# Windowed attention followed by a leaky-ReLU MLP on one core: second heads' dilated values of batch 0 issued by ScalarE, first w_in pieces cast by any of three engines, tables of order remade

## The chip, the core and the metric

The kernel runs on one core of one Trainium2 chip. The core has TensorE (PE, matrix products into PSUM banks), VectorE (DVE), ScalarE (ACT), GpSimd (POOL) and SyncE (SP), each with its own instruction stream in program order. SP, and here ACT too, also issue transfers from main memory. The metric is the device time of one execution in microseconds (us). Three runs of the kernel before gave 295.57, 295.67 and 296.05 us; their median, 295.67 us, is the time before. One more execution was taken with the hardware profiler on.

## What is computed

Attention over 8 batches of 8 heads, 576 positions, 64 values per head, in two kinds of mask, and then a two-layer MLP on the 4608 rows of 512 that come out:

```python
scores = scale * np.matmul(q, k.transpose(0, 1, 3, 2))
rel = pos[:, None] - pos[None, :]
mask_plain = (rel >= 0) & (rel < 32)                          # heads 0 to 3
mask_dil = (rel >= 0) & (rel < 128) & (rel % 4 == 0)          # heads 4 to 7
attn = softmax(np.where(masks, scores, -1e9))                 # last axis
x = np.matmul(attn, v).transpose(0, 2, 1, 3).reshape(4608, 512)
h = x @ w_in                                                  # 512 x 2048
g = np.maximum(0.01 * h, h)
out = g @ w_out                                               # 2048 x 512
```

Inputs and output are float32. The products run on float16 operands.

## The kernel before

**Tiling.** Heads are handled in pairs. A pair is a visit `vi`: visits 2 and 3 hold the dilated heads, 0 and 1 the plain ones, and every batch runs them in the order 2, 3, 0, 1. The two heads of a pair share a 128-partition tile: their keys and values stand in alternate columns of `slots`. A visit is split into two units (`unit`). A unit is a chain: scores on PE into a PSUM bank (`sps`, `ops`), Exp on ACT into `ee` (L904), row sums on PE by a block of ones (L921), Ln and Exp(-x) on ACT into `rc` (L940, L942), values on PE (L915), and a DVE multiply that writes the finished columns into `xt` (L953). For batches 0 and 1 the last 64 positions of all visits are one more unit, the rest unit (`rest_unit`, scores L994, Exp L1012, values L1000).

**Operands.** q, k and v are loaded as float32 into `stg` and `vst`, cast to float16 into `nat` or straight into `slots` (helper `cast`, recorded as L501 on ACT and L502 on DVE and POOL), turned by PE transposes (L740) for batches 0 and 1, and copied from PSUM into `slots` (helper `move`, L513 on ACT, L514 on DVE). The weight `w_in` comes in eight pieces w0 to w7 of 512 KB, one per visit and half of the 2048 columns, `w_out` in eight more, w8 to w15. Each piece is cast in two halves of 512 columns. Until they are cast the pieces stand in buffers that are needed later for something else (`gt`, `wst`, `xt`).

**MLP.** The first layer (`up`, L1054; two 192-column halves together in `up_pair`, L1088) sums four matmuls, one per visit, and ACT writes the leaky ReLU into `gt`. The second layer runs plain for four row tiles (L1268) and then as seven products instead of eight per group of four tiles (`group`, L1358). Chunks 9 to 11 run the first layer in the seven-product form too (L1188).

**What sets the order.** Every piece of work is recorded as a task with one engine or a choice of engines, estimated durations and dependencies. A planner (`_Plan`) schedules all tasks on a model of the machine, forward and backward, eight times, and keeps the best pass. Then each task's rank is moved by its number in `NUDGE`, some tasks are fixed to an engine by `HAND`, and one last forward pass gives the order in which the instructions are written out. `FIRST` sets the rank of the loads of batches 0 and 1 and of the weights. `ROOM`, `LATE`, `SOON`, `FAST` and `WHEN` are constants of the model. On the chip the engines follow the written order and wait for semaphores. Where the plan leaves PE idle before the first `up`, matmuls on the blank tile `warm` are put in (L1589).

**Loads.** `load_v(b, g, prio)` loads a half of the values of a batch: g = 1 the dilated heads, g = 0 the plain ones, `hh` is the first or second head of the pairs. For g = 1 each `hh` takes three transfers, two of 128 KB and one of 32 KB, for g = 0 one of 288 KB in 1152 pieces of 256 bytes. All of these are issued by SP; ACT issues the two halves of the dilated keys of batch 0 and the first constants (`con`). The completion of each transfer is counted on one of eight semaphores taken in turn over both queues, and the planner's model has the same limit:

```python
                    if eng == "SP":
                        here = max(here, landed[-8] if len(landed) >= 8 else 0.0)
```

so a transfer waits on its queue until the one eight places ahead of it in the written order has landed, and everything behind it on that queue waits too.

## Time and profile before

| | before |
|---|---|
| median of three runs | 295.67 us |
| the profiled execution's own time | 296.16 us |
| its span, first to last instruction | 294.4 us |
| PE busy | 284.7 us, 97% of the span |
| PE weight loads busy | 226.3 us, 77% |
| DVE busy | 225.3 us, 77% |
| ACT busy | 218.5 us, 74% |
| POOL busy | 124.2 us, 42% |
| mean granted PE clock | 0.994 of full speed |
| moved by DMA | 47.15 MB, 160 GB/s over the span |

The profile gives busy times per engine and per stretch of time (the windows view), the instructions in order of time (the timeline), who waited for whom (the waits view), groups of instructions of one kind, and the transfers with their time from issue to landing. Times in the views are microseconds from the start of the span; the span is 1.76 us shorter than the profiled execution's own time.

### The profile page before, as it was taken

The numbers are of one execution on the slowest core, as the hardware profiler recorded it, in microseconds if no ns is written. First come the engines' busy times: TensorE is split into PE (matmuls) and PEld (weight loads), VectorE is DVE, ScalarE is ACT, GpSimd is POOL, SyncE is SP. The second block draws the span as 40 slices with busy tenths as digits, with TensorE's granted clock in tenths as the row PEclk, the third lists the DMA queues.
The fourth block names the chain that finished last, engine by engine and source line by source line (L and its number), as shares of the span: only waits on it lengthen the run. The fifth ranks groups of instructions, "written<-read, shape, count | busy, mean of one in ns | idle before, by whom it ended". The sixth has DMA issues, their size and how long they took to land.

```text
span 294.4 us, 7619 instructions
## 1 busy us (share of the span) xinstructions
PE 284.7 (97%) x2920; PEld 226.3 (77%) x2920; DVE 225.3 (77%) x437; ACT 218.5 (74%) x482; POOL 124.2 (42%) x174
## 2 busy tenths in 40 slices
PE   6879999999999999999999999999999999999995
PEld 2557776686687789677777787887688999999984
DVE  7858397864799879867839879897878889678672
ACT  4967898489859985888978887988767965755521
POOL 4540452656537747874873683653424000000000
PEclk9979999999999999999999999999999999999999
DMA  7999999799788969999798898852001210121133
GB/s 240 275 403 401 394 366 203 156 175 208 128 169 185 170 150 186 199 157 199 198 178 142 195 182 153 197 134 75 31 7 36 75 38 0 38 73 36 38 108 109
DMA packets 156068, 47.15 MB, mean 160 GB/s; under 512 B 136832, under 2 KB 153344, under 8 KB 156032
## 3 DMA queue, kind: packets, MB, share of 16 engines
q1 hardware_dynamic: 155344, 46.04, 64.5%
q10 hardware_dynamic: 688, 0.63, 0.6%
q8 instruction: 23, 0.38, 0.5%
q14 instruction: 13, 0.11, 0.1%
HBM read 37.22 MB, written 9.44 MB: 158 GB/s over the span
## 4 chain that ended last, share of the span: by engine, by line
PE 92%; DMA 3%; DVE 2%; ACT 1%; POOL 0%; issue 0%; ACTq 0%; DVEq 0%; SPq 0%
PE hps L1054 27%; PE fps L1358 23%; PE tp L1358 9%; PE hps L1188 5%; PE fps L1268 4%; PE hps L1088 4%; PE ops L1188 3%; PE ops L915 3%; DMA gt<-in_moe_w_in_dram 2%; PE ops L896 2%; PE ops L921 2%; PE sps L896 2%; PE sps L1188 1%; DMA con<-consts 1%; PE sps L921 1%; PE ops L1358 1%
## 5 line engine op out<-in xcount | busy, mean ns | idle before, releaser
L1054 PE MATMUL hps<-xt,w_in 128*128 128x384 f16 x488 | 94.9, 325 | 2.0 <-POOL w_in L502 2.0
L1358 PEld LDWEIGHTS <-gt 128*128 128x128 f16 x768 | 73.0, 98 | 9.8 <-DVE gt L1344 0.2
L1070 ACT ACTIVATE gt<-hps 128x384 f16<-128x384 f32 x122 | 59.1, 488 | 13.6 <-PE hps L1054 12.7
L1054 PEld LDWEIGHTS <-w_in 128*128 128x128 f16 x512 | 45.0, 98 | 23.3 <-POOL w_in L502 2.1
L502 POOL CAST slots<-vst 128x576 f16<-128x576 f32 x55 | 46.7, 875 | 22.8 <-DMA vst<-in_v_dram 6.8
L502 POOL CAST nat<-stg 128x576 f16<-128x576 f32 (+1 forms) x52 | 36.1, 716 | 47.0 <-DVE gt L1344 18.7
L1358 PE MATMUL fps<-w_out,gt 128*128 128x256 f16 x368 | 46.7, 272 | 0.0
L908 DVE TENSOR_TENSOR ee<-ee,con 128x384 f16<-128x384 f16 (+1 forms) x48 | 20.6, 430 | 15.3 <-ACT ee L904 14.8
L942 ACT ACTIVATE rc<-rc 128x288 f32<-128x288 f32 (+1 forms) x64 | 27.2, 437 | 1.1
L953 DVE TENSOR_TENSOR xt<-ops,rc 128x288 f16<-128x288 f32 (+2 forms) x44 | 19.4, 445 | 10.6 <-ACT rc L942 6.1
L513 ACT COPY slots<-turned 64x512 f16<-64x512 f16 (+1 forms) x30 | 23.9, 800 | 0.8 <-DVE turned L705 0.5
L1211 ACT ACTIVATE gt<-vst 128x384 f16<-128x384 f32 (+1 forms) x24 | 16.0, 684 | 8.0 <-DVE vst L1207 8.0
L896 PEld LDWEIGHTS <-slots 128*128 128x128 f16 x308 | 18.2, 98 | 4.8 <-DVE slots L514 0.5
L514 POOL COPY slots<-turned 64x576 f16<-64x576 f16 (+2 forms) x25 | 16.7, 675 | 12.0 <-ACT slots L513 4.3
L904 ACT ACTIVATE ee<-ops 128x416 f16<-128x416 f32 (+2 forms) x35 | 16.7, 487 | 3.7 <-PE ops L896 3.0
L915 PEld LDWEIGHTS <-slots 128*128 128x128 f16 x308 | 17.4, 98 | 2.4 <-ACT slots L501 0.6
L921 PEld LDWEIGHTS <-con 128*128 128x128 f16 x168 | 14.1, 98 | 6.0 <-issue 1.0
L705 DVE STREAM_TRANSPOSE turned<-nat 128x576 f16<-128x576 f16 x24 | 18.0, 759 | 0.1
L904 ACT ACTIVATE ee<-sps 128x416 f16<-128x416 f32 (+2 forms) x29 | 14.4, 497 | 4.2 <-PE sps L896 3.1
L1387 ACT COPY stg<-fps 128x512 f32<-128x512 f32 (+1 forms) x20 | 10.4, 520 | 9.4 <-PE fps L1358 9.0
L1344 DVE TENSOR_TENSOR gt<-gt 128x1024 f16<-128x1024 f16 x21 | 16.6, 791 | 0.3 <-PE fps L1358 0.2
L1188 PEld LDWEIGHTS <-w_in 128*128 128x128 f16 x192 | 16.2, 98 | 0.2
(157 smaller groups left out, 557.8 us busy)
## 6 DMA issues: line engine op xcount, KB each, us to landing
out_dram<-osb SPq DMA_DIRECT2D x32, 256.0 KB, 2.6
stg<-in_k_dram SPq DMA_DIRECT2D x48, 144.0 KB, 3.5
stg<-in_q_dram SPq DMA_DIRECT2D x48, 144.0 KB, 3.6
vst<-in_v_dram SPq DMA_DIRECT2D x16, 288.0 KB, 4.3
vst<-in_v_dram SPq DMA_DIRECT2D x32, 128.0 KB, 3.2
gt<-in_moe_w_in_dram SPq DMA_DIRECT2D x6, 512.0 KB, 7.4
stg<-in_q_dram SPq DMA_DIRECT2D x3, 512.0 KB, 7.0
stg<-in_k_dram SPq DMA_DIRECT2D x3, 512.0 KB, 9.1
```

The lines of the kernel that those rows point to most:

```text
L502: return ENG[e].tensor_copy(out=dst, in_=src)
L513: return nc.scalar.copy(out=dst, in_=src)
L896: nc.tensor.matmul(p_bank[:, c:c + w], slot(tn, KB + 128 * s, 0, 128, [1, 128]), slot(tn, qx, 0, 128, *qd), start=first or not by_pe, stop ...
L904: lambda e: nc.scalar.activation(out=et[:, 0:n], in_=p_bank[:, 0:n], func=AF.Exp, scale=SCALE), prio)
L908: lambda e: nc.vector.tensor_tensor(out=et[:, 0:n], in0=et[:, 0:n], in1=con[:, table:table + n], op=ALU.mult), prio,
L915: nc.tensor.matmul(at(dst, 0, 128, o, *od), lhs(s), et[:, c:c + w], start=i == 0, stop=i == len(steps) - 1, skip_group_check=True)
L921: nc.tensor.matmul(at(p_bank, 0, 128, o, *od), block_ones, at(et, 0, 128, c, *cd), start=i == 0, stop=i == len(rows) - 1, skip_group_check ...
L942: lambda e: nc.scalar.activation(out=rt, in_=rt, func=AF.Exp, scale=-1.0), prio)
L1054: nc.tensor.matmul(ht[:, 0:n], at(w_in, 0, 128, vi * DFF + j // 2 * 256 + j % 2, [2, 128]), at(xt[m % 2], 0, 128, vi * 1152 + x0 + x, [1, n]),
L1070: lambda e: nc.scalar.activation(out=gt[c % NG][:, j * n_c + x:j * n_c + x + n], in_=ht[:, 0:n], func=AF.Prelu, alpha=0.01),
L1188: nc.tensor.matmul(bk[:, n * i:n * i + n], w(v, 2 * z + i), x(v), start=first and i == 0 and v == 0, stop=i == 1 and v == 1, skip_group_ch ...
L1358: nc.tensor.matmul(bk[:, x:x + HN], tl[:, off + j * step:off + j * step + 128], rhs(j), start=first and x == 0 and j == 0, stop=j == HJ - ...
```

## The change

It has three parts. `load_v` issues the three transfers of the second head (`hh` = 1) of the dilated values of batch 0 from ACT's queue instead of SP's. `HELPED` lets ACT, besides POOL and DVE, cast the pieces w0, w1 and w2. And the constants, `FIRST`, `NUDGE` and `HAND` are new; `NUDGE` and `HAND` are numbers by task and are cut here. `SECOND` also changes which PSUM bank the batch-1 transposes of visit 2 use.

```diff
-ROOM, LATE, LANDS, SERVE, FSERVE = 256, 1.06, 0.6, 1.1, 1.04
-SOON = 0
-FAST = 0.21
-WHEN = (3.92, 2.82, 39.64, 80.18, 115.4, 117.81, 161.72, 152.03)
+ROOM, LATE, LANDS, SERVE, FSERVE = 256, 1.26, 0.6, 1.1, 1.04
+SOON = 1
+FAST = 0.22
+WHEN = (4.9, 1.58, 39.5, 80.18, 112.59, 117.81, 123.13, 152.03)
...
-SECOND = 'st01t'
+SECOND = '0t01t'
...
-HELPED = ()
+HELPED = (0, 1, 2)
...
-FIRST = ('r0 q01 q00 v01 v00 w0 w1 w2 w3 w4 w5 w6 q11 w7 w8 q10 w9 w10 v11 w11 w12 w13 w14 v10 '
-         'w15 r1 c')
+FIRST = ('r0 q01 q00 v00 v01 w0 w1 w2 w3 w4 w5 w6 q11 w7 w8 q10 w9 w10 v11 w11 w12 w13 v10 w14 '
+         'w15 r1 c')
 NUDGE = {
...
 HAND = {
...
-    def load_v(b, g, prio, queue="SP"):
+    def load_v(b, g, prio):
...
+            queue = "ACT" if b == 0 and hh else "SP"
             c_in = load(queue, every2(vs, hh, VH * hh + 512, [S, 2], [1, D]),
...
-            ab = [load("SP", every2(vs, hh, VH * hh + j * S, [256, 2], [1, 256]),
+            ab = [load(queue, every2(vs, hh, VH * hh + j * S, [256, 2], [1, 256]),
```

Three places show how instructions move. Lines of the changed kernel are higher by 6 before `load_v` and by 7 behind it.

SP's queue from the plain queries of batch 0 (`stg`, 128x4x256) to the first pieces of `w_in`, before (`vst_73` holds the dilated values, `vst_74` the plain ones):

```order
L486 DMA stg_67<-in_q_dram 128x4x256
L486 DMA vst_73<-in_v_dram 64x2x256
L486 DMA vst_73<-in_v_dram 64x2x64
L486 DMA stg_68<-in_k_dram 128x4x256
L486 DMA vst_73<-in_v_dram 64x2x256
L486 DMA vst_74<-in_v_dram 64x18x64
L486 DMA vst_73<-in_v_dram 64x2x256 x2
L486 DMA vst_73<-in_v_dram 64x2x64
L486 DMA vst_74<-in_v_dram 64x18x64
L486 DMA gt_89<-in_moe_w_in_dram 128x1x1024 x3
```

and now (here `vst_74` holds the dilated values, `vst_73` the plain ones):

```order
L492 DMA stg_67<-in_q_dram 128x4x256
L492 DMA stg_68<-in_k_dram 128x4x256
L492 DMA vst_74<-in_v_dram 64x2x64
L492 DMA vst_74<-in_v_dram 64x2x256
L492 DMA vst_73<-in_v_dram 64x18x64
L492 DMA vst_74<-in_v_dram 64x2x256
L492 DMA vst_73<-in_v_dram 64x18x64
L492 DMA gt_89<-in_moe_w_in_dram 128x1x1024 x3
L492 DMA stg_64<-in_q_dram 128x4x256
L492 DMA gt_90<-in_moe_w_in_dram 128x1x1024
```

Three transfers of values have left SP's queue ahead of w0, two of 128 KB and one of 32 KB. A load of batch-1 queries now stands between w2 and w3. Ahead of these rows the last-64 keys and queries now come first and the dilated queries of batch 0 behind them.

ACT's stream around the Exp of the plain visits of batch 0 (`ee`, from `sps` and `ops`), with the Ln and the Exp(-x) of the units in `rc`, before:

```order
L942 ACTIVATE rc_83<-rc_83 128x256
L513 COPY slots<-fps_106 64x512
L940 ACTIVATE rc_84<-sps_104 128x288
L904 ACTIVATE ee_80<-ops_101 128x320
L942 ACTIVATE rc_84<-rc_84 128x288
L904 ACTIVATE ee_81<-sps_104 128x416
L940 ACTIVATE rc_85<-ops_101 128x224
```

and now:

```order
L519 COPY slots<-fps_106 64x512
L911 ACTIVATE ee_79<-sps_104 128x416
L947 ACTIVATE rc_83<-ops_101 128x256
L507 CAST w_in<-gt_89 128x512
L947 ACTIVATE rc_84<-sps_104 128x288
L949 ACTIVATE rc_83<-rc_83 128x256
L911 ACTIVATE ee_80<-ops_101 128x320
L949 ACTIVATE rc_84<-rc_84 128x288
L507 CAST w_in<-gt_89 128x512
L947 ACTIVATE rc_85<-ops_101 128x224
L911 ACTIVATE ee_81<-sps_104 128x416
```

ACT now casts one half each of w0, w1 and w2 (the third cast follows two rows on), between the Ln and Exp of the plain visits. Of the other halves DVE casts those of w0 and w2 and POOL that of w1; before, POOL and DVE cast one half each.

PE's stream where the two units of batch 1's visit 0 have their scores (L896 on `slots`) and their row sums (L921 on `ee`), before:

```order
L896 MATMUL ops_100<-slots 128x96
L896 LDWEIGHTS slots
L896 MATMUL ops_100<-slots 128x64
L921 LDWEIGHTS con
L921 MATMUL ops_101<-ee_80,con 128x5x32
```

and now, with the first of the rows that have come in between:

```order
L903 MATMUL ops_101<-slots 128x96
L903 LDWEIGHTS slots
L903 MATMUL ops_101<-slots 128x32
L1095 LDWEIGHTS w_in
L1095 MATMUL hps_102<-xt_86,w_in 128x192
```

Eight such matmuls of 192 columns of the first layer (L1088 before) now stand between the scores and the row sums that wait for their Exp, and the sums of the smaller unit come first; before, the sums followed the scores directly.

14 lines of the change are left out of this document (8 added, 6 removed), and 160 rows, old and new, of the table NUDGE.

## The prediction

> **What bounds the kernel now.** I read the windows view first, in long stretches and then by the microsecond where PE is not full (columns: busy time and instruction count of PE, PE weight loads, DVE, ACT, POOL; then granted PE clock, DMA share, GB/s).
>
> ```profile
> 25.00:291.00 266.00, 265.65 (x2728) 214.49 (x2724) 207.70 (x403) 201.43 (x443) 113.71 (x155) 1.00 0.63 145
> ...
> 12.00:13.00 1.00, 1.00 (x18) 0.73 (x16) 0.97 (x2) 1.00 (x3) 0.84 (x1) 1.00 0.52 129
> 14.00:15.00 1.00, 0.69 (x10) 0.37 (x9) 0.95 (x3) 1.00 (x4) 0.33 (x2) 1.00 0.71 229
> 16.00:17.00 1.00, 0.67 (x14) 0.44 (x10) 0.90 (x2) 1.00 (x5) 0.00 (x0) 1.00 1.02 397
> 17.00:18.00 1.00, 0.00 (x0) 0.00 (x0) 0.19 (x1) 0.53 (x1) 0.16 (x1) 1.00 1.01 410
> 19.00:20.00 1.00, 1.00 (x10) 0.76 (x9) 0.43 (x1) 0.57 (x2) 0.87 (x1) 0.52 1.04 410
> 20.00:21.00 1.00, 1.00 (x7) 0.48 (x6) 0.47 (x2) 0.50 (x2) 0.62 (x1) 0.50 1.02 414
> 21.00:22.00 1.00, 1.00 (x15) 0.86 (x12) 0.33 (x1) 0.57 (x2) 0.00 (x0) 0.50 0.99 402
> 22.00:23.00 1.00, 1.00 (x12) 0.70 (x11) 0.35 (x2) 0.64 (x3) 0.00 (x0) 0.78 1.07 391
> ```
>
> From 25 us to 291 us PE is idle for 0.35 us in all: there the kernel is PE's own work, and the change alters no matmul of it (it only alters the warm fillers of the opening and the banks of some transposes). So whatever the opening gains moves the end by as much, unless it is given back. The opening has two losses. PE stands still around 17 us, and right behind that its clock is halved for some 3.5 us: 0.48 + 0.50 + 0.50 + 0.22 = **1.70 us** of full-speed work lost. The waits view names the standstill and the one wait left in the long stretch; the timeline gives the places.
>
> ```profile
> PE hps L1054 <- POOL w_in L502: 2.0, 1, 2.0
> PE ops L921 <- ACT ee L904: 0.3, 1, 0.3
> ...
> 11.82 0.40 PE L740 MATMUL tp<-con,nat 128*128 128x128 f16 x4 [0.69 <-ACT nat L501]
> 18.77 0.34 PE L1054 MATMUL hps<-xt,w_in 128*128 128x384 f16 x1 [2.01 <-POOL w_in L502]
> 24.77 0.53 PE L1000 MATMUL ops<-ee,slots 128*128 128x16 f16 x14
> 34.09 1.46 PE L1054 MATMUL hps<-xt,w_in 128*128 128x384 f16 x8
> 35.39 0.39 PE L740 MATMUL ops<-con,nat 128*128 128x128 f16 x4
> ```
>
> The first `up` starts at 18.77, after POOL's cast of w0. The values of batch 0's rest unit (L1000, 24.77) are my **anchor**: in both orders they stand behind the last attention unit of batch 0, with PE full from there on. The changed order has one more 384-column matmul ahead of them; it costs (35.39 - 34.09) / 8 = 0.16. The gain of the opening is therefore 24.77 + 0.16 less the anchor's new time.
>
> **When w0 comes.** The timeline of SP's and ACT's queues and of ACT, the transfers' answers (x1: one transfer, KB, us to landing) and POOL's first cast of w_in:
>
> ```profile
> 11.78 2.67 SPq L486 DMA_DIRECT2D gt<-in_moe_w_in_dram  x4
> 17.80 0.54 SPq L486 DMA_DIRECT2D wst<-in_moe_w_in_dram  x1
> 0.76 1.00 ACTq L486 DMA_DIRECT2D stg<-in_k_dram  x2
> 3.88 1.14 ACT L501 CAST nat<-stg 128x512 f16<-128x512 f32 x2 [1.87 <-DMA stg<-in_q_dram]
> ...
> gt<-in_moe_w_in_dram SPq DMA_DIRECT2D x1, 512.0 KB, 6.0
> vst<-in_v_dram SPq DMA_DIRECT2D x1, 288.0 KB, 3.6
> ...
> 17.84 0.87 POOL L502 CAST w_in<-gt 128x512 f16<-128x512 f32 x1 [2.09 <-DMA gt<-in_moe_w_in_dram]
> ```
>
> w0 is issued at 11.78 and lands at 17.78; the transfer eight places behind it goes out at 17.80, so the limit of eight binds. Taking three transfers off SP would save 3 x 0.67 (2.67 / 4) = 2.0 us of issuing, the bound above. But in the new order w0 waits for the second of ACT's value transfers to land. ACT issues that one behind its cast of the first keys (two casts took it from 3.88 to 5.02; one, with the keys as the later of the two inputs, to about 4.9) and one issue of 0.5, so about 5.4, and at the 3.6 to 6.0 us of the rows it lands at 9.0 to 11.4. So w0 is issued 0.4 to 2.0 us earlier and, at its old 6.0 us, lands at 15.8 to 17.4.
>
> (The Trainium skill, "Trainium Kernel Development and Optimization", section Key Constraints, says that queues of different engines share the same 16 DMA engines and that issuing from several only saves issue time. The rows at 12 and 14 us, shares of 0.52 and 0.71, show 0.8 us of unused DMA; by that rule w0 comes 0.8 us earlier, at 17.0.)
>
> Anywhere in that range it does not matter: what is late next is ACT.
>
> **ACT's chain in the opening.** These rows carry the largest term.
>
> ```profile
> 6.80:17.50 10.70, 8.37 (x102) 5.44 (x100) 9.14 (x19) 10.07 (x24) 4.62 (x6) 1.00 0.98 310
> ...
> L501 ACT CAST slots<-vst 128x576 f16<-128x576 f32 x4 | 3.5, 868 | 0.0
> L942 ACT ACTIVATE rc<-rc 128x256 f32<-128x256 f32 x4 | 1.7, 443 | 0.0
> L513 ACT COPY slots<-fps 64x512 f16<-64x512 f16 x2 | 1.5, 729 | 1.8 <-PE fps L740 1.8
> L501 ACT CAST nat<-stg 128x512 f16<-128x512 f32 x1 | 0.6, 617 | 0.0
> L513 ACT COPY slots<-tp 128x512 f16<-128x512 f16 x1 | 0.6, 586 | 0.2 <-PE tp L740 0.2
> ...
> 5.15 0.54 DVE L507 MEMSET slots<- 128x576 f32 x1
> 5.61 0.36 DVE L502 CAST nat<-stg 128x512 f16<-128x512 f32 x1
> 7.56 0.74 DVE L514 COPY slots<-fps 64x512 f16<-64x512 f16 x1 [0.29 <-ACT slots L513]
> 8.33 0.29 DVE L502 CAST rest<-stg 128x256 f16<-128x256 f32 x1
> 6.80 0.73 ACT L513 COPY slots<-fps 64x512 f16<-64x512 f16 x1 [1.78 <-PE fps L740]
> ```
>
> Before, ACT's copies out of PSUM begin at 6.80, and 24 instructions take 10.07 us of union up to 17.5. *Start.* Now DVE blanks one tile more (0.54) before its first cast at 5.61, casts a piece of `rest` (0.29) and makes its first copy (0.74), for which ACT's first copy waits, since both read one bank: 5.61 + 0.54 + 0.29 + 0.74 + 0.1 of hand-over = 7.3. ACT's own three issues (1.5 us from 4.9) and its second key cast (0.62) end about 7.0 and hide under that. *The next 24* are again 24, with three 64x512 copies and one 128x512 copy more, two value casts, one `nat` cast and one Exp(-x) less: 3 x 0.729 + 0.586 - 2 x 0.868 - 0.617 - 0.443 = -0.02. So 10.07, and 0.5 for two waits on DVE that I find in the walk (its three rest copies, its upper half of the last key copy): 7.3 + 10.1 + 0.5 = 17.9. w0 is there by then, with 0.5 to 2.1 us to spare; if it came as before, at 17.79, that would still hold. *The first cast* on ACT, at the 0.617 of the `nat` cast of equal size: the first `up` at **18.5**, 0.25 earlier than before. HELPED's gain of POOL's 0.87 against 0.62 is inside this; its price is three casts in a chain that is now the limit.
>
> *To the anchor* ACT has 14 more: three casts, three Ln, four Exp(-x), four Exp, up to the rest unit's own Exp. At the mean of 10.07 / 24 = 0.42 they take 5.9. Bound below: the short activations, eleven of them, start 0.31 apart when nothing waits.
>
> ```profile
> 9.99 0.38 ACT L940 ACTIVATE rc<-sps 128x256 f32<-128x256 f32 x1
> 10.53 0.72 ACT L942 ACTIVATE rc<-rc 128x256 f32<-128x256 f32 x2
> 11.14 0.62 ACT L501 CAST nat<-stg 128x512 f16<-128x512 f32 x1
> 11.65 0.84 ACT L501 CAST slots<-vst 128x576 f16<-128x576 f32 x1
> ```
>
> From 9.99 to 11.14 four of them (one Ln is left out here) take 1.15, or 0.29 each; the cast takes 0.51 to the next start. With the wider Exps at up to 0.39: 3 x 0.51 + 11 x 0.31 = 4.9. So the anchor lies at 17.9 + 4.9 + 0.2 = 23.0 to 17.9 + 5.9 + 0.2 = 24.0. I take 23.75, near the slower end, because each Ln and each sum crosses between PE and ACT. **Gain of the opening: 24.93 - 23.75 = 1.2**, bounds 0.9 and 1.9.
>
> That holds the clock at full. Before, a pause of 2.01 was followed by half speed, and one of 0.69 (11.82) was not: the rows at 12 and 14 us show 1.00. In my walk the longest pause before the first `up` is some 0.85 (at 14.7, for the last keys' bank), the rest 0.3 or less, with fillers between.
>
> **The long stretch.** The wait of 0.3 on Exp at batch 1's visit 0 goes: eight matmuls of 192 columns now stand in between, as much as four of 384, 4 x 0.16 = 0.65 us, twice the wait. Gain 0.3, bound below 0. The later w_in pieces come behind two loads of batch 1, but by the columns of the matmuls ahead of them their first use is 7.5 us of PE work past the anchor; the two loads come earlier. I cost the rest of the remade ranks at nothing; what hides them is the 266 us of PE work with 0.35 idle, and a rank that leaves PE without work would cost that wait.
>
> ```profile
> 30.00:40.00 10.00, 10.00 (x96) 7.28 (x94) 5.03 (x10) 9.31 (x22) 5.88 (x10) 1.00 1.06 395
> ```
>
> **Sum.** 1.2 + 0.3 = 1.5 against the profiled span of 294.4 gives 292.9. The execution itself took 296.16, 1.76 around the span; 0.49 above the median. I take the difference to the median: 295.67 - 1.5 = **294.2**. Its own range, by the bounds: 293.5 to 294.8.
>
> **Rivals.** *The clock is halved again* (20%): the pauses between 13 and 18 us are enough though none is long. That gives back up to 1.70: 295.9. (The Trainium skill, "TensorE: Matmul & The Clock Gate", section on the HAM clock gate, has half clock after an idle window of about 3.4 us. Here 2.01 us of pause was followed by it, so pauses well under that figure are no safety; the halved stretch of some 3.5 us does agree.) Against it: the 0.69 row.
>
> *Given back behind the opening* (13%): PE arrives 1.2 us earlier at 30 to 40 us, where ACT is busy 9.31 of 10. If ACT sets the pace there, the opening's gain goes and 0.3 is left: 295.4. Against it: PE waits for ACT nowhere in that stretch before.
>
> *ACT's chain is the new wait, and slower* (12%): if ACT's starts don't overlap its ends, because each step waits for PE or DVE, an activation costs its full 0.44 (L942), not the 0.29 between starts. With half of the 38 steps so: 19 x 0.15 = 2.85, anchor 26.6, 1.7 late, less 0.3: 297.1. It decides from an anchor past 25.2. For it: more of ACT's copies now alternate with DVE's on one bank. Against it: so they did before, in 10.07.
>
> **Chances.** The forecast 55%, the three rivals 20, 13 and 12. A change within 0.2% (0.59 us) can't be told from none. Faster by more: the forecast and the better ends of the first two rivals, 0.62. Within: 0.23. Slower: 0.15, the last rival and a halved clock that lasts longer. The range reaches from just under the forecast's best end to past the halved clock: 293.2 to 296.1.
>
> **What would show it.** The first `up` at 18.5 with ACT's cast as its releaser, not a transfer; granted clock 1.00 from 16 to 24 us; L1000 at 23.75; no wait on Exp of batch 1's visit 0; PE idle under 0.5 us from 25 us on. Wrong: a clock of 0.5 anywhere behind 6 us, w0 landing after 17.9, L1000 past 24.9, or new PE waits between 25 and 60 us.

## The result, and the profile after

The changed kernel takes **297.71 us** (297.63 to 297.92, four executions); the kernel before, beside it on the same chip, 295.62 (294.88 to 296.05, four). The ratio is 1.0074 with a 95% interval of 1.0053 to 1.0095: slower by about 2.1 us. The forecast was 294.2, faster. The profiled execution of the changed kernel took 297.69 us, its span is 295.9.

The windows view of the changed kernel, with the columns as in the prediction:

```profile
25.00:291.00 266.00, 264.61 (x2713) 213.34 (x2711) 202.90 (x388) 205.00 (x457) 110.66 (x154) 1.00 0.64 146
...
7.00:8.00 1.00, 0.00 (x0) 0.00 (x0) 0.70 (x2) 0.15 (x1) 0.00 (x0) 1.00 1.05 339
...
18.00:19.00 1.00, 0.50 (x5) 0.21 (x4) 0.94 (x3) 1.00 (x3) 0.00 (x0) 1.00 0.94 369
...
20.00:21.00 1.00, 1.00 (x15) 0.64 (x12) 0.42 (x1) 1.00 (x5) 0.04 (x1) 1.00 1.11 404
21.00:22.00 1.00, 1.00 (x15) 0.68 (x13) 0.79 (x2) 1.00 (x4) 0.00 (x0) 1.00 0.99 371
```

Two things are to be seen. The granted clock is 1.00 throughout, where the profiled execution before had 0.50. And from 25 to 291 us PE is idle for 266.00 - 264.61 = 1.39 us, where it was 0.35. The waits view says for whom, and the timeline where (of the waits, those of L1061 and of L903 lie behind 25 us, the others in the opening):

```profile
PE tp L747 <- DVE nat L508: 2.0, 1, 2.0
...
PE hps L1061 <- ACT gt L1108: 0.7, 1, 0.7
PE sps L928 <- ACT ee L911: 0.7, 2, 0.3
PE fps L747 <- ACT slots L519: 0.7, 1, 0.7
PE ops L928 <- ACT ee L911: 0.5, 1, 0.5
PE ops L903 <- DVE xt L960: 0.4, 2, 0.2
PE ops L899 <- ACT rc L947: 0.4, 1, 0.4
PE hps L1061 <- ACT gt L1077: 0.3, 1, 0.3
```

```profile
8.83 0.40 PE L747 MATMUL tp<-con,nat 128*128 128x128 f16 x4 [2.04 <-DVE nat L508]
19.88 0.32 PE L1061 MATMUL tp<-xt,w_in 128*128 128x384 f16 x1
24.83 0.53 PE L1007 MATMUL ops<-ee,slots 128*128 128x16 f16 x14 [0.18 <-ACT ee L1019]
33.28 0.32 PE L1061 MATMUL hps<-xt,w_in 128*128 128x384 f16 x1 [0.68 <-ACT gt L1108]
75.86 0.32 PE L1061 MATMUL hps<-xt,w_in 128*128 128x384 f16 x1 [0.31 <-ACT gt L1077]
105.92 0.27 PE L903 MATMUL ops<-slots 128*128 128x64 f16 x3 [0.18 <-DVE xt L960]
119.21 0.33 PE L903 MATMUL ops<-slots 128*128 128x96 f16 x5 [0.22 <-DVE xt L960]
...
4.52 3.29 ACTq L492 DMA_DIRECT2D vst<-in_v_dram  x3
7.85 0.62 ACT L507 CAST nat<-stg 128x512 f16<-128x512 f32 x1 [3.44 <-DVE rest L508]
8.38 0.72 ACT L519 COPY slots<-fps 64x512 f16<-64x512 f16 x1
19.20 0.61 ACT L507 CAST w_in<-gt 128x512 f16<-128x512 f32 x1
24.23 0.55 ACT L1019 ACTIVATE ee<-sps 128x448 f16<-128x448 f32 x1 [0.26 <-PE sps L1001]
...
7.26 0.29 DVE L508 CAST rest<-stg 128x256 f16<-128x256 f32 x1 [0.97 <-DMA stg<-in_q_dram]
7.59 0.73 DVE L520 COPY slots<-fps 64x512 f16<-64x512 f16 x1
```

The first `up` starts at 19.88 (18.77 before), the anchor at 24.83 (24.77 before, with one matmul of 0.16 us less ahead of it). So the opening gained 0.1 us although it no longer loses 1.70 us to a halved clock. From the anchor to the end of the span it is 295.9 - 24.83 = 271.07 us, before 294.4 - 24.77 = 269.63: with the 0.16 that moved ahead, **1.60 us are lost behind the anchor**. As idle time of PE only 0.82 of them show (271.07 - 266.74 = 4.33 us behind the anchor, 269.63 - 266.12 = 3.51 before); the other 0.78 are PE time that counts as busy, and no view says what it waited for. These two numbers, the anchor and the rest of the span, serve for every run below.

Of 107 executions of the kernel before that stand beside the experiments, 18 had a mean granted clock of 0.994 (median 296.20 us) and 89 had 0.998 or more (median 294.66): the halved clock that its profiled execution shows comes in one execution in six, and these executions are 1.5 us longer. Three executions counted as slow (298.38 and 759.73 us of the kernel before, 762.22 of e6) are left out of these counts and of the ratios below.

### The profile page after: what moved, and what is told of

Same layout as the page of the kernel before. It is cut to its first block, busy times and chain, and to the rows that moved or that the text cites. A ratio compares the mean times of both kernels' runs of the same rounds, so it can differ in the third digit from the quotient of the medians.

```text
span 295.9 us, 7626 instructions
## 1 busy us (share of the span) xinstructions
PE 285.1 (96%) x2926; PEld 226.7 (77%) x2926; DVE 219.7 (74%) x423; ACT 223.8 (76%) x499; POOL 119.4 (40%) x171
## 4 chain that ended last, share of the span: by engine, by line
PE 82%; ACT 9%; DVE 4%; DMA 2%; issue 2%; SPq 0%; DVEq 0%
PE hps L1061 25%; PE fps L1365 21%; PE tp L1365 7%; PE hps L1195 5%; PE fps L1275 4%; PE ops L1195 3%; PE hps L1095 3%; ACT slots L519 3%; PE ops L922 2%; DMA stg<-in_q_dram 2%; PE ops L903 2%; PE sps L1195 1%; PE sps L903 1%; ACT rc L947 1%; PE ops L928 1%
## 5 line engine op out<-in xcount | busy, mean ns | idle before, releaser
L1061 PE MATMUL hps<-xt,w_in 128*128 128x384 f16 x488 | 93.9, 325 | 1.0 <-ACT gt L1108 0.7
L1061 PEld LDWEIGHTS <-w_in 128*128 128x128 f16 x512 | 45.5, 98 | 23.5 <-issue 1.4
L508 POOL CAST slots<-vst 128x576 f16<-128x576 f32 x59 | 50.4, 887 | 21.8 <-DMA vst<-in_v_dram 4.4
L508 POOL CAST nat<-stg 128x576 f16<-128x576 f32 (+1 forms) x50 | 33.4, 682 | 40.4 <-DVE gt L1351 14.1
L915 DVE TENSOR_TENSOR ee<-ee,con 128x384 f16<-128x384 f16 (+1 forms) x48 | 19.7, 416 | 9.9 <-ACT ee L911 9.2
L519 ACT COPY slots<-turned 64x512 f16<-64x512 f16 (+1 forms) x31 | 25.0, 805 | 0.6
L1394 ACT COPY stg<-fps 128x512 f32<-128x512 f32 (+1 forms) x23 | 12.2, 529 | 12.5 <-PE fps L1365 12.0
L903 PEld LDWEIGHTS <-slots 128*128 128x128 f16 x308 | 18.1, 98 | 4.5 <-issue 0.7
L520 POOL COPY slots<-turned 64x64 f16<-64x64 f16 (+2 forms) x28 | 17.1, 612 | 9.6 <-DVE ee L915 4.3
L1218 ACT ACTIVATE gt<-vst 128x768 f16<-128x768 f32 (+1 forms) x24 | 16.1, 683 | 4.0 <-DVE vst L1214 3.8
L947 ACT ACTIVATE rc<-ops 128x288 f32<-128x288 f32 (+2 forms) x35 | 13.6, 397 | 3.7 <-PE ops L928 3.5
```

What stands on the lines that cost most here:

```text
L508: return ENG[e].tensor_copy(out=dst, in_=src)
L519: return nc.scalar.copy(out=dst, in_=src)
L903: nc.tensor.matmul(p_bank[:, c:c + w], slot(tn, KB + 128 * s, 0, 128, [1, 128]), slot(tn, qx, 0, 128, *qd), start=first or not by_pe, stop ...
L915: lambda e: nc.vector.tensor_tensor(out=et[:, 0:n], in0=et[:, 0:n], in1=con[:, table:table + n], op=ALU.mult), prio,
L1061: nc.tensor.matmul(ht[:, 0:n], at(w_in, 0, 128, vi * DFF + j // 2 * 256 + j % 2, [2, 128]), at(xt[m % 2], 0, 128, vi * 1152 + x0 + x, [1, n]),
```

## The experiments

To move single tasks without touching the others, the planner's last pass is replaced in most runs by a table of its own result: for each task its engine and its place in the written order.

```diff
-    order = plan.run()
+    order = listed(plan)
```

Rows with + and - below are instructions of one engine in that order. "Old" and "new" stand for the orders before and after.

| run | median us | before beside it | ratio, 95% interval | anchor | span less anchor |
|---|---|---|---|---|---|
| profiled before | | | | 24.77 | 269.63 |
| profiled after | 297.71 | 295.62 | 1.0074 (1.0053 to 1.0095) | 24.83 | 271.07 |
| e1 | 305.40 | 294.85 | 1.0361 (1.0335 to 1.0388) | 25.02 | 278.58 |
| e2 | 306.50 | 294.85 | 1.0404 (1.0370 to 1.0438) | 22.94 | 281.36 |
| e3 | 297.11 | 294.85 | 1.0085 (1.0058 to 1.0111) | 25.16 | 270.04 |
| e4 | 294.84 | 294.85 | 1.0004 (0.9987 to 1.0022) | 23.22 | 269.68 |
| e5 | 297.67 | 294.38 | 1.0119 (1.0096 to 1.0141) | 24.78 | 271.02 |
| e6 | 296.33 | 294.38 | 1.0065 (1.0043 to 1.0087) | 24.92 | 269.58 |
| e7 | 294.38 | 294.38 | 0.9997 (0.9978 to 1.0017) | 23.17 | 269.53 |
| e8 | 297.59 | 294.38 | 1.0116 (1.0092 to 1.0140) | 25.58 | 271.12 |
| e9 | 297.80 | 295.16 | 1.0086 (1.0056 to 1.0115) | 24.68 | 271.12 |
| e10 | 297.48 | 295.16 | 1.0076 (1.0046 to 1.0105) | 24.70 | 271.30 |
| e11 | 296.62 | 295.16 | 1.0059 (1.0032 to 1.0086) | 24.65 | 271.65 |
| e12 | 294.75 | 295.16 | 0.9987 (0.9963 to 1.0011) | 23.05 | 269.85 |
| e13 | 297.53 | 295.05 | 1.0079 (1.0049 to 1.0109) | 24.12 | 271.08 |
| e14 | 294.66 | 295.05 | 0.9983 (0.9964 to 1.0001) | 22.72 | 269.68 |
| e15 | 305.47 | 295.05 | 1.0338 (1.0307 to 1.0369) | 25.03 | 279.07 |
| e16 | 296.92 | 295.04 | 1.0075 (1.0049 to 1.0102) | 23.92 | 271.08 |
| e17 | 296.49 | 295.04 | 1.0044 (1.0013 to 1.0075) | 24.77 | 270.53 |
| e18 | 296.93 | 294.56 | 1.0081 (1.0053 to 1.0109) | 23.65 | 271.15 |

Anchor and span are from the one profiled execution of each run. Where the order behind the anchor is the changed one (the profile after, e5, e8, e9, e10, e13, e16, e18) the part behind it lies between 271.02 and 271.30; e11 alone has 271.65. The anchor itself moves more, because the first loads land differently each time: e16 and e17 have one and the same order up to it, and theirs are 23.92 and 24.77. A difference of a few tenths between two anchors therefore shows nothing by itself.

### Opening or what is behind it: e1, e2, e5, e6, e11

**e1 and e2** glue the two orders together at the anchor: the table is the new one up to it and the old one behind it, or the reverse.

> The changed kernel up to the values of batch 0's rest unit (all three parts of the change in the opening), and behind them every task in the order and on the engine of the kernel before. Theory 1 (what was lost lies in the order behind the anchor, where PE now waits for ACT and DVE, 1.6 us in all): about 295.5 us, the 0.1 us that the opening gained. Theory 2 (the opening leaves the machine in a state, late loads and late casts, that causes the waits whatever the order behind it): near the changed kernel, 297.2 to 297.7 us.

> The kernel before up to the values of batch 0's rest unit, and behind them every task in the order and on the engine of the changed kernel. Theory 1 (the order behind the anchor costs 1.6 us by itself): 297.0 to 297.5 us, with PE waits on ACT near 33, 76 and on DVE near 106 and 119 us, and the old wait at 49.7 gone. Theory 2 (the waits come from the opening's late loads): 295.2 to 295.8 us.

Both missed by some 8 us and more, for a reason of their own: the loads of w4 to w8 were issued ahead of the anchor in one order and their casts stood behind it in the other. The timeline of DVE in e1 shows the price there:

```profile
32.02 0.76 DVE L508 CAST w_in<-wst 128x512 f16<-128x512 f32 x2 [6.69 <-DMA wst<-in_moe_w_in_dram]
```

They say nothing on the question, but that the order of loads and of casts belong together. **e6 and e11** repeat them with the loads from w4 on, those of batch 1 and their casts all on the far side of the cut. **e5** is the changed kernel once more. (The stalls in the texts of e6, e11 and e15 are the time from the anchor to the end of the span less PE's work there, about 267.8 us: 1.7 before, 3.4 after.)

> The changed kernel itself, unaltered, beside more executions of the kernel before. If the kernel before runs here mostly at a granted clock of 1.00 (294.85 us), as it did beside the first four experiments, while its profiled execution had 0.994 (1.70 us of work at half clock): the changed kernel, which holds 1.00 in any case, should be slower by 2.5 to 3.1 us here instead of the 2.1 us of the result. Rival (the difference between two groups of runs of the kernel before has nothing to do with its clock): 2.1 us again.

> Once more the changed kernel's opening with the old order behind it, now with the loads from w4 on, the batch-1 loads and their casts in the old order too, so that no piece of w_in is cast in another order than it is loaded. Theory 1 (1.7 us are lost by the order behind the anchor): PE work still to be done behind the anchor finishes with 1.7 us of stalls in place of 3.4, and the time is 296.0 us (the changed kernel's 297.7 less 1.7). Theory 2 (the waits come from the opening): 297.2 to 297.7 us.

> Once more the old opening with the changed order behind the anchor, with the loads from w4 on, the batch-1 loads and their casts in the new order too. Theory 1 (the new order behind the anchor costs 1.8 us of stalls by itself: 3.4 in place of 1.7): 296.0 to 296.4 us beside 294.4 for the kernel before, with PE stalls near 31, 74, 104 and 118 us. Theory 2 (those stalls follow from the new opening): 294.2 to 294.8 us.

e5 is 3.3 us slower than the kernel before (294.38, which here had the lower clock in 3 of 17 executions), not 2.1. e6, new opening and old rest, is 1.9 us slower and its part behind the anchor is 269.58, the old figure. e11, old opening and new rest, is 1.5 us slower by the medians and its part behind the anchor is 271.65, 2.0 more than the old one (and 0.6 more than the changed kernel's, which stays open; its executions spread from 295.65 to 298.92). The two ratios, 1.0065 and 1.0059, multiply to 1.0124; e5 has 1.0119. **So there are two losses, about equal, and they add up.** At full clock the old anchor lies at 23.22 (e4), with the matmul more 23.38: the new opening is 24.83 - 23.38 = 1.45 us slower, or 1.40 to 1.78 by the profiles of e5, e6 and e3, which have the same opening (24.78, 24.92, 25.16).

### The halved clock: e4

```diff
+    up_at = next(i for i, t in enumerate(order) if t.kind == "U")
+    for _ in range(8):
+        w = _Task((("PE", 0.2),), [], idle(512), 0, 0.0, 0, "w", False, None)
+        w.eng, w.start, w.dur = "PE", order[up_at].start, 0.2
+        order.insert(up_at, w)
```

> The kernel before with eight matmuls of 512 columns on a blank tile put ahead of the first matmul of the first layer, in the pause of 2.01 us in which PE waits for w0; nothing else is changed. Theory (the pause halves the clock for the 3.5 us behind it, 1.70 us of work lost): granted clock 1.00 from 17 to 24 us and 294.0 us, 1.6 less than before. Rival (ACT or DVE sets the pace behind the first matmul of the first layer, so that the clock costs little): 295.0 to 295.6 us.

The windows view of e4 in the place of the pause:

```profile
17.00:18.00 1.00, 1.00 (x10) 0.49 (x7) 0.86 (x3) 0.93 (x3) 0.48 (x1) 1.00 0.94 373
18.00:19.00 1.00, 1.00 (x8) 0.50 (x6) 0.49 (x2) 0.00 (x0) 0.60 (x2) 1.00 0.99 401
19.00:20.00 1.00, 1.00 (x15) 0.73 (x13) 0.19 (x1) 0.73 (x3) 0.66 (x1) 1.00 1.04 397
```

The pause is filled, the clock is 1.00 and the anchor comes at 23.22 in place of 24.77: against the profiled execution before, the gain is the 1.55 us that were expected. The median does not move, because most executions of the kernel before keep the full clock too. Neither theory had that. All 12 executions of e4 had 0.999 or more, and so had the 36 of e7, e12 and e14, whose first `up` comes without that pause; of the kernel before 18 in 107 had 0.994. In e11's profiled execution the pause of 2.00 is there and the clock is 0.50 behind it. The pause is not the same in every execution: in e2's, whose queue of SP is the old one up to 17 us, w0 was issued at 11.46 and landed 5.1 later in place of 11.78 and 6.0, the pause is 0.73 and the clock stays at 1.00. How long it was in the 107 executions is not on record.

### The parts of the change alone: e7, e9, e10

```diff
-    def load_v(b, g, prio, queue="SP"):
+    def load_v(b, g, prio):
...
+            queue = "ACT" if b == 0 and hh else "SP"
             c_in = load(queue, every2(vs, hh, VH * hh + 512, [S, 2], [1, D]),
...
-            ab = [load("SP", every2(vs, hh, VH * hh + j * S, [256, 2], [1, 256]),
+            ab = [load(queue, every2(vs, hh, VH * hh + j * S, [256, 2], [1, 256]),
```

> The kernel before with the first part of the change alone: the three transfers of the second head's dilated values of batch 0 on ACT's queue, behind its two casts of the first keys; all else in the old order. Theory (SP's queue is what makes w0 late: three issues fewer, 0.8 us each in the trace): w0 lands 1 to 2 us earlier, the first matmul of the first layer starts at 17 to 17.8 us, and the time is 293.6 to 294.4 us. Rival (the 16 DMA engines are full, so w0 lands when it did, and ACT is held up by its own issues): 294.8 to 295.6 us.

The timeline of e7 (SP's queue, PE, DVE):

```profile
10.58 3.48 SPq L486 DMA_DIRECT2D gt<-in_moe_w_in_dram  x4
...
17.29 0.34 PE L1055 MATMUL hps<-xt,w_in 128*128 128x384 f16 x1
23.17 0.54 PE L1001 MATMUL ops<-ee,slots 128*128 128x16 f16 x14 [1.02 <-DVE xt L954]
...
21.99 0.76 DVE L502 CAST w_in<-gt 128x512 f16<-128x512 f32 x2 [1.27 <-DMA gt<-in_moe_w_in_dram]
22.66 0.45 DVE L954 TENSOR_TENSOR xt<-ops,rc 128x288 f16<-128x288 f32 x1
```

In the old order the first part of the change does what it is for: w0 goes out at 10.58 in place of 11.78 and the first `up` starts at 17.29, 1.5 us earlier than in the profile before. (Some of that is the execution's: with the same edit w0 goes out at 11.11 and 11.08 in e12 and e14, without it at 11.46 to 11.99 in the profiles before and of e2, e4 and e11, and e2's first `up` starts at 17.25.) But 1.02 us are given back at one place: the anchor waits for a DVE multiply that stands behind the casts of w3, and w3 lands at 21.99. The time is the same.

**e9** undoes the same edit in the changed kernel (the three issues go from ACT's stream to SP's).

> The changed kernel with its first part undone: the three transfers of the second head's dilated values of batch 0 on SP's queue, at their place in the written order; ACT still casts halves of w0, w1 and w2, and all ranks are the new ones. Theory (ACT's queue, blocked from 4.5 to 7.85 us by these issues, starts its chain late): ACT's first copy out of PSUM starts near 7.5 us in place of 8.4 and the anchor and the end come 0.5 to 0.9 us earlier, 296.8 to 297.2. Rival (DVE's cast for the rest unit, which waits for its load until 7.26 us, holds the same copy just as long, and w0 comes later behind three more issues on SP): no gain, 297.5 to 298.5 us.

The timeline of e9:

```profile
7.11 0.29 DVE L508 CAST rest<-stg 128x256 f16<-128x256 f32 x1 [0.81 <-DMA stg<-in_q_dram]
7.43 0.73 DVE L520 COPY slots<-fps 64x512 f16<-64x512 f16 x1
...
8.20 0.73 ACT L519 COPY slots<-fps 64x512 f16<-64x512 f16 x1 [0.72 <-DVE slots L520]
```

The rival holds: ACT is free now, and its first copy waits for DVE's copy from the same bank, which stands behind a cast for the rest unit whose load lands at 7.11. No gain. **e10** takes the three casts of w_in off ACT; of POOL's stream:

```diff
-L508 CAST w_in<-gt_89 128x512
+L508 CAST w_in<-gt_89 128x512 x3
```

> The changed kernel with its second part undone: the half of w0, of w1 and of w2 that ACT casts goes to POOL, DVE and POOL, at the same places in the written order; everything else as changed. Theory (ACT's chain sets the anchor, and these three casts take 0.51 us each of it): the anchor up to 1.0 us earlier and 296.6 to 297.1 us. Rival (POOL's cast of w0, 0.87 us, and the waits of the other engines take the place): 297.4 to 298.2 us.

The anchor comes 0.13 earlier, and the time can't be told from the changed kernel's. The two halves of the opening say more. The first `up` starts at 20.13, 0.25 later than in the changed kernel, although ACT's first copy starts 0.42 earlier, at 7.96; from there to the anchor it is 24.70 - 20.13 = 4.57 us, and 24.83 - 19.88 = 4.95 in the changed kernel (4.95 again in e5, 4.96 in e8 and e9). So the three casts on ACT cost 0.38 us there, too little to show in the time.

### What holds the opening: e8, e13, e16, e18

**e8** has the dilated queries first on SP again, and DVE's casts in that order:

```diff
+L492 DMA stg_65<-in_q_dram 128x2x256
 L492 DMA stg_64<-in_k_dram 64x8x64
+L492 DMA stg_65<-in_q_dram 128x2x256
 L492 DMA stg_64<-in_q_dram 64x8x64
-L492 DMA stg_65<-in_q_dram 128x2x256 x2
```

> The changed kernel with the dilated queries of batch 0 first on SP's queue again, ahead of the last-64 keys and queries, and DVE's casts of them ahead of those for the rest unit; nothing else is moved. Theory A (the queries' late loads, for whose cast PE waits 2.04 us at 8.8 us, set the opening back): the first matmul of the first layer 0.8 to 1.2 us earlier, at 18.7 to 19.1 us, and the anchor by as much. Theory B (ACT's queue, blocked by its three value issues until 7.85 us, sets it back): the wait of PE shrinks, but the first matmul of the first layer moves by less than 0.3 us.

PE's wait of 2.04 for the queries is gone, one of 1.9 for the rest unit's casts has come, and the first `up` and the anchor are 0.74 and 0.75 later: neither theory. (e5 settles the wait itself: there it is 0.96, as seven matmuls on the blank tile ahead of it took 2.51 us in place of 1.67, and the anchor is where it was.) The timeline of ACT in e8 names the other holder: its own three issues block it until 8.9.

```profile
4.52 4.37 ACTq L492 DMA_DIRECT2D vst<-in_v_dram  x3
8.93 0.62 ACT L507 CAST nat<-stg 128x512 f16<-128x512 f32 x1 [3.97 <-issue]
```

So ACT's first copy is held in two ways at once: by DVE's copy, behind the cast for the rest unit, and by ACT's own issues. In the changed kernel the two end at 8.32 (7.59 + 0.73) and 8.47 (7.85 + 0.62), and e8 and e9 each took one of them away. Both hang on one landing, that of the last-64 queries, which the new order issues at 1.51. The transfers' answer of the changed kernel (KB, us from issue to landing):

```profile
stg<-in_q_dram SPq DMA_DIRECT2D x1, 128.0 KB, 5.7
```

DVE's cast waits for it, and so does ACT's third value issue, which stands eight places behind it and goes out at 7.19; in e5, e6 and e10 the issue and the cast move together, at 7.14 and 7.22, 7.28 and 7.36, 6.79 and 6.86. In e8 DVE's copy is out of the way, but ACT's hold grew: its second issue waits in the same way for the last-64 keys, until 7.62. **e13** takes both away, and more with them: everything up to the row sums of the first visit, and all loads of batch 0, in the old order. ACT's stream:

```diff
-L492 DMA vst_74<-in_v_dram 64x2x256 x2
-L492 DMA vst_74<-in_v_dram 64x2x64
-L507 CAST nat_70<-stg_66 128x2x4x64
 L519 COPY slots<-fps_106 64x512
 L519 COPY slots<-tp 128x4x128
+L911 ACTIVATE ee_79<-sps_104 128x320
+L911 ACTIVATE ee_80<-ops_101 128x320
+L519 COPY slots<-fps_105 64x2x64
 L519 COPY slots<-fps_106 64x512
```

> The changed kernel whose first 9 us are the old ones: everything up to the row sums of batch 0's first visit, and all loads of batch 0, stand in the order and on the queue and engine of the kernel before (so the second head's values are back on SP's queue); from there on everything is in the new order. What it tells apart: whether the 1.5 us that the new opening is slower lie in its start or in what comes behind it. Theory (they lie in the start: ACT's first copy at 8.4 us in place of 6.8 and the first Exp at 10.97 in place of 8.71, after which ACT is busy without a gap): the anchor comes 1.0 to 1.5 us earlier and the time is 296.2 to 296.8 us. Rival (ACT's chain behind the first Exp is longer by its copies and by the casts of w_in, whatever the start): 297.3 to 297.8 us.

ACT's first copy starts at 6.65 in place of 8.38, the first `up` at 19.18, 0.70 earlier, and the anchor at 24.12, 0.71 earlier: half of the 1.45, and less than half of the 1.73 at the start. From the first copy to the anchor it takes 17.47 us here and 16.45 in the changed kernel, so ACT's chain gives the rest back. The time, 297.53, is the rival's. PE's longest wait is now behind the first Exp, for a Ln on ACT:

```profile
11.82 0.30 PE L899 MATMUL ops<-con 128*128 128x192 f16 x2 [1.71 <-ACT rc L947]
```

**e16** adds what follows on ACT. (The lag in the texts of e16 and e18 is the anchor's time less PE's own work ahead of it, about 9.4 us: 24.12 is a lag of 14.7.)

```diff
+L947 ACTIVATE rc_83<-sps_104 128x256
+L947 ACTIVATE rc_84<-ops_101 128x256
 L519 COPY slots<-fps_106 64x512
 L519 COPY slots<-fps_105 64x2x64 x2
-L947 ACTIVATE rc_84<-ops_101 128x256
```

> The run with the old first 9 us once more, and on ACT the two Ln of batch 0's first visit moved ahead of the copies out of PSUM that the new order has in front of them; nothing else. In that run PE waited 1.71 us at 11.8 us for one of these Ln, behind three copies (1.24 us). Theory (the other half of the opening's loss is this order on ACT): the wait falls to 0.5 to 0.9 us, the anchor comes 0.4 to 0.8 us earlier (its lag behind PE's work 14.0 to 14.3 in place of 14.7) and the time is 296.7 to 297.1. Rival (ACT is full from there to the anchor, so that what is moved ahead is paid by what it passes): the wait goes, the anchor stays within 0.2 us, 297.3 to 297.7.

The wait goes, the first `up` comes 0.43 earlier and the anchor 0.20. By the anchor that is nearly the rival, by the time, 296.92, it is the theory; e17, with the same opening, has an anchor of 24.77, so one profile doesn't decide it. ACT is busy almost without a gap from there to the anchor (0.44 us ahead of the rest unit's Exp), which fits the rival: what is put ahead is paid by what it passes. **e18** takes the casts of w_in off ACT as well, as in e10.

> The old first 9 us and the two Ln ahead of the copies, as in the run before last, and the halves of w0, w1 and w2 that ACT casts on POOL, DVE and POOL. What it tells: alone, taking these casts off ACT moved the anchor by 0.13 us. Theory (ACT's chain holds the anchor with several links, so that one link taken out shows little and two show more): the lag of PE behind its work at the anchor 14.0 to 14.2 in place of 14.5 (13.96 in the old order at full clock), the time 0.3 to 0.5 us less than with the casts on ACT, 296.4 to 296.6 us. Rival (POOL's slower cast of w0 gives it back): lag 14.5, 296.8 to 297.2 us.

From the first `up` to the anchor it is 23.65 - 19.08 = 4.57 us again, as in e10, and the anchor comes another 0.27 earlier, although ACT's first copy starts later than in e16, at 7.18 in place of 6.59; the time, 296.93, doesn't show it and is inconclusive. By these single anchors the links together make 24.83 - 23.65 = 1.18 of the 1.45 us. Of the links only the 0.38 of the casts repeats between profiles; what the others carry, and the last 0.27, stay open.

### What holds the long stretch: e3, e17, e15

**e3** moves two copies of batch 1's first turned visits from ACT back to DVE; ACT's stream:

```diff
-L519 COPY slots<-tp 128x4x128
 L1108 ACTIVATE gt_89<-hps_103 128x2x192
 L519 COPY slots<-ops_100 64x512
-L519 COPY slots<-tp 64x512
 L1108 ACTIVATE gt_89<-hps_102 128x2x192
```

> The changed kernel with two copies of batch 1's first turned visits (128x512 and 64x512, out of the transposes' bank into slots) back on DVE, as before the change; ACT had taken them over and made them ahead of two leaky ReLUs for which PE waited 0.84 us at 33.3. Theory 1 (such copies on ACT make the waits): the stall at 33.3 goes and the time falls by 0.6 to 0.8 us, to 296.9 to 297.1. Rival (ACT is short of time in this whole stretch, and the next wait takes the place): the stall goes but the others grow, 297.5 to 297.8 us.

The part behind the anchor falls from 271.07 to 270.04, 1.03 less; at the place itself PE now starts the next product at 32.98 without a wait in the view (0.68 before), and of the two waits of L903 for DVE's multiplies one is left. The median is 0.6 below the changed kernel's; the ratio can't be told from its own. **e17** is e16 with the same two copies:

> The same with the two copies of batch 1's first turned visits back on DVE, as in the third experiment, where that took 0.6 us off the stall near 33 us and the gain stayed to the end. Theory (the losses are separate and add up): 0.6 us less than the run beside it. Rival (the stall is cured but a later one grows): the same time as the run beside it.

0.43 us less than e16 by the medians (the intervals overlap) and 271.08 to 270.53 behind the anchor: no later stall grew. **e15** leaves the new order alone and gives each task behind the anchor its old engine, 91 moves; the first of ACT's stream are those of e3, and these:

```diff
-L519 COPY slots<-ops_101 128x512
-L1077 ACTIVATE gt_88<-hps_103 128x384
-L519 COPY slots<-ops_100 64x512
+L1077 ACTIVATE gt_88<-hps_103 128x384
```

> The changed kernel, every task in its new place in the written order, but behind the values of batch 0's rest unit each task on the engine that had it before the change (91 tasks, most of them copies that went from DVE to ACT or were swapped between POOL, ACT and DVE). What it tells apart: whether the 1.8 us of new stalls behind the anchor come from the choice of engines or from the order. Theory A (the engines: ACT took over work): stalls behind the anchor fall from 3.4 to about 1.7 us and the time is 296.0 us. Theory B (the order: products of the first layer stand too close to the leaky ReLU that frees their bank, and copies stand ahead of it): 297.3 to 298.0 us, with the stall at 33.3 gone, since it hangs on two copies that ACT took over, and those near 76, 106 and 119 us still there.

Neither theory: 305.47 us, and 279.07 behind the anchor. PE is idle for 9.46 us behind the anchor (4.33 in the changed kernel); the longest waits there in the view are again PE's for DVE's multiplies.

```profile
PE ops L903 <- DVE xt L960: 1.2, 2, 0.8
PE ops L1195 <- DVE vst L1214: 0.8, 1, 0.8
PE ops L928 <- ACT ee L911: 0.6, 2, 0.5
PE ops L928 <- POOL ee L936: 0.6, 1, 0.6
```

By this run engine and place of a task can't be judged apart: each table is a solution of its own, and the places of one with the engines of the other cost 8 us more than the slower of the two.

### A better version: e12, e14

**e12** is e7 with DVE's casts of w3 and w7 behind the multiplies:

```diff
+L954 TENSOR_TENSOR xt_86<-ops_100,rc_83 128x288
 L502 CAST w_in<-gt_90 128x512 x2
-L954 TENSOR_TENSOR xt_86<-ops_100,rc_83 128x288
+L954 TENSOR_TENSOR xt_86<-hps_103,rc_84 128x224
 L502 CAST w_in<-wst_96 128x512 x2
-L954 TENSOR_TENSOR xt_86<-hps_103,rc_84 128x224
```

> The kernel before with the first part of the change alone, as in the run before of that kind, and with one thing more: on DVE the two casts of w3, which wait for its landing until 21.99 us, and those of w7 stand behind the multiplies that write the last attention columns of batch 0, instead of ahead of them. In that run the anchor waited 1.02 us for such a multiply. Theory (the 1.2 us that the earlier w0 gains at the first matmul of the first layer were given back at that one wait): the wait goes, and the time is 293.3 to 293.7 us against 294.4. Rival (w3 itself, landing at 22 us, is the next wait, since the first layer needs it right behind the anchor): 294.0 to 294.5 us.

The wait of 1.02 is gone, yet the profiled anchor is 23.05: in this execution ACT waited 1.09 us for a load of values at 13.1, which in e7 was there (0.83 in e14's profile); the time, 294.75, fits neither text. **e14** also moves one pair of products from 38 us to the row sums of batch 1's visit 0:

```diff
 L897 MATMUL ops_100<-slots 128x64
+L1089 LDWEIGHTS w_in
+L1089 MATMUL hps_102<-xt_86,w_in 128x192
```

> The kernel before with the values of the second head on ACT's queue and the casts of w3 and w7 behind the last multiplies of batch 0, as in the run before, and with one pair of 192-column products of the first layer (eight matmuls) taken from 38 us to the place between the scores and the row sums of batch 1's visit 0, its leaky ReLU behind the Exp(-x) there; this is what the changed order does at that place. Theory: the wait of 0.47 us there goes and nothing takes its place: PE's last matmul 0.4 to 0.5 us earlier against its work than in the kernel before at full clock, 294.0 to 294.6 us beside 294.4 to 295.2 for the kernel before, and a full clock in every execution. Rival (the products are missed at 38 us, where scores then wait for DVE's copies): no gain over the run without this move.

The wait at the row sums went, and a new one came where the products were missed, as its rival said:

```profile
40.57 0.31 PE L893 MATMUL ops<-con 128*128 128x192 f16 x2 [0.34 <-DVE slots L514]
```

e12 and e14 stand at 0.9987 and 0.9983 of the kernel before, with intervals that reach 1.0011 and 1.0001: no version was shown to be faster than the kernel before.

## Why the prediction was wrong, step by step

**PE bounds the kernel behind the opening: right as a reading, wrong as a licence.** "I cost the rest of the remade ranks at nothing; what hides them is the 266 us of PE work with 0.35 idle" is the step that failed most clearly. An engine with 0.35 us of idle time in 266 has no slack in which a wait could hide: each wait that a new place brings is added to the time. The new places cost 1.60 us in the profile and 2.0 in e11, and two copies of them, moved from DVE to ACT, 1.03 of it in e3.

**The base of the opening.** The 24.77 from which its gain was counted belongs to an execution with the halved clock. "0.48 + 0.50 + 0.50 + 0.22 = 1.70" is right for that execution (e4: 1.55), but one execution in six has a halved clock, so that most of this gain was not to be had against the median. Which of the four executions beside the result had it isn't known.

**w0.** Forecast: issued 0.4 to 2.0 us earlier, landing at 15.8 to 17.4. It was issued at 12.28, half a us later than before, and landed 5.8 later, at 18.1; the rows of the changed kernel's queue and of that transfer:

```profile
7.31 4.92 SPq L492 DMA_DIRECT2D vst<-in_v_dram  x5
12.28 2.12 SPq L492 DMA_DIRECT2D gt<-in_moe_w_in_dram  x3
```

Five transfers of values took SP 4.92 us, and ACT's three took 3.29 in place of the 1.5 of the forecast. A single issue took 0.60 to 0.77 us on either queue; the rest is waits for the transfer eight places ahead to land. ACT's third went out at 7.19, as the last-64 queries landed, and SP's fourth at 10.93, as ACT's first value transfer landed (issued at 4.52, 6.4 on its way). That limit was named, and applied to w0 alone. Here w0's lateness cost nothing: DVE's cast of it starts at 19.11 without a wait. In the old order the same edit did bring w0 out earlier (e7, e12 and e14).

**ACT's chain: the length right, the start wrong.** Forecast: first copy at 7.3, first cast of w_in 10.6 later, the rest unit's Exp 4.9 to 5.9 behind it. Measured: 8.38; 19.20 - 8.38 = 10.82; 24.23 + 0.55 - 19.20 = 5.58. In the sum's own terms the miss of the anchor, 24.83 in place of 23.75, is the 1.08 us of the start; the two terms behind it are off by 0.2 each way and cancel. The sum for the start lacked the landing of the last-64 queries, which holds DVE's cast for the rest unit (0.97 us of wait) and ACT's issues, thought hidden, as well. That the lengths came out right is in part luck: with the old start (e13) the chain takes 1.02 longer and the anchor gains only 0.71. How much of the 1.45 the start alone carries stays open.

**The clock** stayed at 1.00, as forecast; the rival with the halved clock fell. But the reason given, no pause over some 0.85, did not hold: PE paused for 2.04 us up to 8.8, and the clock stayed full all the same. By the forecast's own row, a pause of 2.01 followed by half speed, that was luck.

**The wait at batch 1's visit 0** went, as forecast.

**The rivals.** "Given back behind the opening" named the place (30 to 40 us), the engine (ACT) and the sort of wait; there it was 0.68 in the view, and it was not the only one. Its reason, that PE arrives earlier, was not what happened. "ACT's chain is the new wait, and slower" has the anchor: 1.45 us later at equal clock, though not for its reason, since the steps of the chain kept their length. Each had 12 or 13%; the two together make the result, and no case of the forecast had both.

## What to carry to other kernels

A written order in which the busiest engine is idle for a third of a us in 266 has no slack behind it: cost a remade table at the waits it may make, not at the busy time that seems to hide it. Count a gain against the median of several executions' clocks, not against the one that was profiled. And if a chain's start is held by two things of equal length, undoing either alone shows nothing: look for what both wait for, and take both away before a cause is ruled out.

## What was not expected of the hardware

Behind PE's pause of 2.01 us ahead of the first `up` the granted clock was 0.50 for some 3.4 us in the profiled execution before, and again behind the pause of 2.00 in e11's; with the pause filled (e4) it was 1.00. Of 107 executions of the kernel before 18 had the lower clock, against none of the 48 of e4, e7, e12 and e14. Pauses of 2.04, 2.32, 2.33 and 2.47 us that end between 8.8 and 9.2 us, in the profiles after and of e3, e6 and e15, were all followed by 1.00. So the length of a pause alone does not decide it. Whether the other 89 executions had as long a pause, or a shorter one as in e2 (0.73), is not known. (The Trainium skill, "TensorE: Matmul & The Clock Gate", section on the HAM clock gate, says that the window of some 3.4 us in which activity is watched runs freely, so that the same kernel differs from run to run: that would fit, but pauses that differ from run to run would fit as well. Its bound, no idle gap over 3.4 us, was not enough here.)

An issue of a transfer took ACT 0.46 to 0.49 us at the start and 0.62 to 0.72 for the three of the values. When one had to wait for an earlier transfer to land, all of ACT waited with it: from the first to the last of the three it was 3.29 us (4.37 in e8), and ACT's next cast started at 7.85 (8.93).
